# Halves of the first and last pair's keys, scored as they land, in a one-core decode attention kernel

## The chip, the core and the metric

The kernel runs on one core of a Trainium2 chip. A core has five engines with instruction streams of their own: TensorE (PE in the profile), VectorE (DVE), ScalarE (ACT), GpSimd (POOL) and SyncE (SP), which issues nearly all the loads here. Loads go through 16 DMA engines. The metric is the time of one execution in device microseconds, as a median over runs: 693.17 us for the kernel before (three runs, 692.98 to 693.86).

## The reference

One token goes through a conditioned transformer block: a modulated layer norm, attention of 32 heads over a cache of 16384 tokens, the output matrix wo, a second modulated layer norm, and a gated feed-forward part. Cut to what matters:

```python
mod = (_silu(c) @ w_mod).reshape(1, 6, 1, -1)          # sa, ca, ga, sb, cb, gb
h = _layernorm(x) * (1 + ca) + sa
q = (h @ wq)                                           # 32 heads of 128
scores = einsum('bhqd,bhkd->bhqk', q, k_cache) * 128 ** -0.5   # 16384 tokens a head
o = einsum('bhqk,bhkd->bhqd', softmax(scores), v_cache)
x = x + ga * (o @ wo)
h = _layernorm(x) * (1 + cb) + sb
x = x + gb * ((_silu(h @ w_gate) * (h @ w_up)) @ w_down)
```

Everything is bf16; keys and values are 268 MB of the 290 MB that are read.

## The kernel before

**Pairs of heads.** The 32 heads are taken as 16 pairs. Partition `(h q)` of the 128 holds one of the pair's two heads and one of 64 blocks of 256 tokens (`T2 = 256`), so a pair's keys are a tile of 128 partitions x 256 tokens x 128 values, 8.4 MB. Keys live in `kring`, two such buffers used in turn; values in the single buffer `vbuf`. In the text, K0 to K15 and V0 to V15 are the loads of pairs 0 to 15.

**Loads.** All large loads are issued by SP, one after the other on one queue, each after a wait of its own: the keys of pair p + 1 once PE has summed the scores of pair p - 1 (`load_k`, `o_R`), the values of pair p once PE has used those of pair p - 1 (`load_v`, `o_pv`). The order is w_mod, wq, K0, K1, V0, K2, V1, K3, V2 and so on to K15, V14, then wo (two loads, into the first key buffer), V15 in four pieces (`VCUT`), and w_gate, w_up, w_down (into the second key buffer).

**Scores of a pair** (`step`, `score`, `reduce_mm`). DVE multiplies the keys in place by the query (L481), adds the two halves of the 64 products it took (L485, a fold), and folds again (L490). It does so for one half of each row's 128 values (all 256 tokens), then for the other. PE sums what remains over an identity matrix into a PSUM tile: 16 matmuls of 256 columns for each half (L472), 32 in all. So DVE can start a pair only when all its keys have landed.

**Weights and values.** While DVE works on pair p, the scores of pair p - 1 go through their maximum (`largest`: DVE L494, ACT L496, PE L498) and exponentials (`weigh`: DVE L502, ACT L506), and PE multiplies them with the values (`pv`, L445, 64 matmuls), ACT copies the sums (L451), and PE takes out the diagonal blocks (`diag`, L460), which ACT stores as `OT_sb` (L465).

**The tail.** After pair 15's scores come its maximum and weights, a sum of all weights over partitions (L570), its reciprocal (L572), the product with the heads' outputs (L573), a spread of these over columns (`z_op`, L589) and a small matmul with a copy (`lay`, L602, L605) that brings them into the layout of wo's rows, 140 matmuls with wo for the first 28 heads (`project`, L617), the values of pair 15, its diagonal, and 20 matmuls for the last four heads. Then follow the second layer norm, w_gate and w_up (L661) and w_down (L682), and the store.

**Order.** Each engine works in the order in which the program is written. On PE alone, pairs 2 to 15 form a hardware loop of seven rounds with two pairs each (`in_loop`); within it each wait is a semaphore count that grows by a fixed step per round.

Of the kernel before, what the change touches and what calls it, by code (L numbers as in the profile page):

```python
# [8 lines left out]
ALU = mybir.AluOpType  # L9
# [4 lines left out]
class _Chan:  # L14

    def __init__(self, sem, inc):
        self.sem = sem
        self.inc = inc
        self.count = 0

# [16 lines left out]
class _Plan:  # L37
# [54 lines left out]
    def emit(self, block):  # L92
# [5 lines left out]
        for e in self.ENGS:  # L98
            by_place = {}
            for o in per_eng[e]:  # L100
                if o.loop:
                    key, i, n = o.loop
                    by_place.setdefault((key, i), []).append(o)
            for (key, i), ops in by_place.items():
                first = by_place[(key, 0)]
                assert len(first) == len(ops), (key, i)
                for a, b in zip(first, ops):
                    a.sig = a.sig or b.sig
            for (key, i), ops in by_place.items():
                for a, b in zip(by_place[(key, 0)], ops):  # L110
                    b.sig = a.sig
            for o in per_eng[e]:
                if o.sig:
                    ch = o.chan if o.chan is not None else self.chans[e]
                    o.chan = ch
                    ch.count += ch.inc
                    o.val = ch.count
# [7 lines left out]
        def run(name, eng):  # L125
            known = {}
            ops = per_eng[name]
            at = 0
            while at < len(ops):
# [16 lines left out]
                done = {}  # L146
                with eng.Fori(0, n) as it:
                    for b in range(body):
                        each = [self.needs(r[b]) for r in rows]
                        assert all(set(x) == set(each[0]) for x in each), rows[0][b].name  # L150
                        for k, (ch, v0) in each[0].items():
                            step = each[1][k][1] - v0
                            assert all(x[k][1] == v0 + j * step for j, x in enumerate(each)), (rows[0][b].name, [x[k][1] for x in each])
                            if known.get(k, 0) >= each[-1][k][1]:
                                continue
                            if k in done and done[k][1] == step and done[k][0] >= v0:
                                continue
                            done[k] = (v0, step)
                            assert v0 > 0 and step >= 0
                            eng.wait_ge(ch.sem, v0 if step == 0 else it * step + v0)  # L160
                        issue(eng, rows[0][b])
# [28 lines left out]
def build(nc, A_x, A_k, A_v, A_wq, A_wo, B_wg, B_wu, B_wd, c_in, w_mod, out):  # L190
# [20 lines left out]
    with es:  # L211
# [265 lines left out]
        def score(p, c, between=None):  # L477
# [4 lines left out]
                     deps=[d_k[p]] + o_qev[p // 2], name="mult%d_%d" % (p, c))  # L482
# [4 lines left out]
            if between:  # L487
# [3 lines left out]
                      deps=[o_f], name="fold%d_%db" % (p, c))  # L491

# [17 lines left out]

        def step(p):
            f0 = score(p, 0, (lambda: largest(p - 1), lambda: weigh(p - 1)) if p >= 1 else None)
            reduce_mm(p, 0, f0)
            if p >= 1:
                pv(p - 1)
            o_R[p] = reduce_mm(p, 1, score(p, 1))
            if p >= 1:
                diag(p - 1)
# [4 lines left out]
        step(0)  # L523
        load_k(2)
        step(1)
        load_v(1)
        NLOOP = (NP - 2) // 2
        d_wo = {}
        for p in range(2, NP):
            plan.in_loop(LOOP_ON, "pairs", (p - 2) // 2, NLOOP)  # L530
            if p + 1 < NP:
                load_k(p + 1)
            else:
                a = 0
                while a < len(GROUPS):
                    b = a
                    while b < len(GROUPS) and GROUPS[b][1] == GROUPS[a][1]:
                        b += 1
                    (h0, n), h1 = GROUPS[a], GROUPS[b - 1][0] + GROUPS[b - 1][1]
                    d = dma(wo_v[:, h0:h1, :].rearrange("p (g k) n -> p g (k n)", k=n),  # L540
                            A_wo[h0 * 128:h1 * 128, :].rearrange("(g p k) n -> p g (k n)", p=128, k=n),
                            ("wo", a), deps=[o_R[NP - 2]], name="dma_wo%d" % a)
                    for i in range(a, b):
                        d_wo[i] = d
                    a = b
# [8 lines left out]
        wdeps = [o_R[NP - 1]]  # L554
        d_wg = dma(wg_v, B_wg.rearrange("(p k) n -> p k n", p=128), "wg", deps=wdeps, name="dma_wg")
        wu_src = B_wu.rearrange("(p k) n -> p k n", p=128)
        UK = KC - 1
        d_wu = [dma(wu_v[:, 0:UK, :], wu_src[:, 0:UK, :], "wu0", deps=wdeps, name="dma_wu0"),
                dma(wu_v[:, UK:KC, :], wu_src[:, UK:KC, :], "wu1", deps=wdeps, name="dma_wu1")]
        d_wd = []  # L560
        for b in range(NB):
            d_wd.append(dma(wd_v[:, 4 * b:4 * b + 4, :].rearrange("p r n -> p (r n)"),
                            B_wd[512 * b:512 * b + 512, :].rearrange("(p r) n -> p (r n)", r=4), ("wd", b), deps=wdeps, name="dma_wd%d" % b))
        d_wd.append(dma(wd_v[0:FR, 4 * NB:FCH, :].rearrange("p r n -> p (r n)"),
                        B_wd[512 * NB:F, :].rearrange("(p r) n -> p (r n)", r=2), ("wd", NB), deps=wdeps, name="dma_wd%d" % NB))

        LAST = H - 2
        o_Lm = op(PE, lambda e: e.matmul(misc[:, LS0:LS0 + H], lhsT=ones_f[:], rhs=rsz[:], start=True, stop=True),  # L570
                  deps=[o_exp[NP - 1], o_rz, o_onesf, o_rstd], name="L")
        o_rl = op(DVE, lambda e: e.reciprocal(out=rl[:], in_=misc[:, LS0:LS0 + H]), deps=[o_Lm, o_ones1], name="rl")  # L572
        o_on = op(DVE, lambda e: e.tensor_tensor(out=on_f[:, 0:LAST], in0=OT_sb[:, 0:LAST], in1=rl[:, 0:LAST], op=ALU.mult),  # L573
                  deps=[o_rl] + o_ot[0:NP - 1], name="on")
        zoff, zo = [], 0
        for h0, n in GROUPS:
            zoff.append(zo)
            zo += 1
# [45 lines left out]
        for g in range(NG - 1):  # L624
            project(g)

        pv(NP - 1)
# [108 lines left out]
```

## Time and profile before

| | us |
|---|---|
| median of 3 runs | 693.17 |
| the profiled execution | 693.76 |
| its span, by the trace | 692.0 |
| DVE busy | 504.7 (73%) |
| PE busy | 384.1 (55%) |
| ACT busy | 45.8 (7%) |
| data read | 290.47 MB, 420 GB/s over the span |

The span is that of the profiled execution; the numbers worked out from rows below belong to it. In a row of a group of instructions stand line, engine, operation, output and input with their shapes and the count, then the busy time and the mean ns of one, then the idle time of the engine just before them and what ended it. A row of the chain has start, duration and what ran. A row of a window has its bounds and length, the busy time of PE, weight load, DVE, ACT and POOL, the granted clock of TensorE, the mean busy share of the DMA engines and GB/s. A row of loads issued ends with the size in KB and the time from issue to landing in us.

### The profile page before, as it was taken

How to read it: one execution, taken by the hardware profiler on the slowest of the kernel's cores; microseconds unless marked ns; L12 is line 12 of the kernel's file. 1: busy time of each engine (PE TensorE's matmuls, PEld its weight loads, DVE VectorE, ACT ScalarE, POOL GpSimd, SP SyncE). 2: the span in 40 equal slices, each digit the busy share in tenths (PEclk: the TensorE clock that was granted, in tenths of full speed). 3: DMA queues.
4: the chain of work that ended last, by engine and by line, in shares of the span. 5: the costliest groups of instructions: out<-in, count | busy, mean ns of one | idle time of the engine just before them, and what ended most of it. 6: DMA issues, size and time to landing. Idle time of an engine off the chain costs nothing.

```text
span 692.0 us, 5102 instructions
## 1 busy us (share of the span) xinstructions
PE 384.1 (55%) x2280; PEld 154.2 (22%) x2281; DVE 504.7 (73%) x174; ACT 45.8 (7%) x145; POOL 0.7 (0%) x6
## 2 busy tenths in 40 slices
PE   2523457745728284745728184645738173746786
PEld 2311112221302122221212122221212121221355
DVE  2029999959596896959596986959595987959311
ACT  1120000000000000000000000000000000000100
POOL 0000000000000000000000000000000000000000
PEclk9975556565556555565655565655556565555665
DMA  9999899999999999999999999999999999999993
GB/s 388 438 424 425 367 424 417 425 428 426 425 428 462 428 432 432 424 428 447 443 428 432 428 424 428 466 424 428 432 428 424 439 455 428 428 432 404 416 421 120
DMA packets 7135, 290.63 MB, mean 420 GB/s; under 512 B 882, under 2 KB 884, under 8 KB 1876
## 3 DMA queue, kind: packets, MB, share of 16 engines
q1 hardware_dynamic: 7120, 290.48, 97.6%
q8 instruction: 8, 0.13, 0.1%
q14 instruction: 3, 0.02, 0.0%
q10 hardware_dynamic: 4, 0.00, 0.0%
HBM read 290.47 MB, written 0.00 MB: 420 GB/s over the span
## 4 chain that ended last, share of the span: by engine, by line
DMA 45%; DVE 41%; PE 12%; ACT 1%; issue 1%; SPq 0%; DVEq 0%
DMA kring<-in_A_k_cache_dram 45%; DVE kring L481 22%; DVE kring L485 11%; PE psb L472 8%; DVE kring L490 6%; PE psb L617 1%; PE psb L661 1%; PE psb L445 1%; PE psb L682 0%; DVE pm L494 0%; PE psb L460 0%; DVE nb L502 0%; ACT PZ L506 0%; PE psb L602 0%; SPq L79 0%
## 5 line engine op out<-in xcount | busy, mean ns | idle before, releaser
L481 DVE TENSOR_TENSOR kring<-kring,qbc 128x16384 bf16<-128x16384 bf16 x32 | 278.0, 8687 | 126.5 <-DMA kring<-in_A_k_cache_dram 126.5
L472 PE MATMUL psb<-kring,ident 128*128 128x256 bf16 x512 | 225.6, 607 | 159.5 <-DVE kring L490 159.5
L485 DVE TENSOR_TENSOR kring<-kring 128x8192 bf16<-128x8192 bf16 x32 | 141.4, 4420 | 0.6
L472 PEld LDWEIGHTS psb<-kring,ident 128*128 128x128 bf16 x512 | 59.2, 121 | 308.5 <-DVE kring L490 171.2
L445 PE MATMUL psb<-vbuf,PZ 128*8 128x512 bf16 x1024 | 87.9, 516 | 0.5 <-PE psb L445 0.5
L498 PE MATMUL psb<-d,bd_f 128*128 128x64 f32 x32 | 11.0, 447 | 115.7 <-ACT d L496 115.7
L490 DVE TENSOR_TENSOR kring<-kring 128x4096 bf16<-128x4096 bf16 x32 | 73.1, 2286 | 0.6
L445 PEld LDWEIGHTS psb<-vbuf,PZ 128*8 128x8 bf16 x1024 | 28.5, 108 | 64.7 <-issue 55.3
L498 PEld LDWEIGHTS psb<-d,bd_f 128*128 128x128 f32 x32 | 8.0, 310 | 117.9 <-ACT d L496 64.4
L460 PEld LDWEIGHTS psb<-sel,acc_sb 128*128 128x128 f32 x128 | 29.4, 319 | 7.5 <-issue 4.6
L460 PE MATMUL psb<-sel,acc_sb 128*128 128x2 f32 x128 | 26.2, 327 | 0.7 <-ACT acc_sb L451 0.7
L451 ACT ACTIVATE acc_sb<-psb 128x512 f32<-128x512 f32 x16 | 9.6, 597 | 216.0 <-PE psb L445 216.0
L506 ACT ACTIVATE PZ<-psb,nb 64x256 bf16<-64x256 f32 x32 | 15.0, 468 | 63.0 <-DVE nb L502 62.8
L496 ACT ACTIVATE d<-negid,pm 128x64 f32<-128x64 f32 x16 | 5.6, 348 | 151.1 <-DVE pm L494 150.9
L408 PE MATMUL psb<-vbuf,h_col 128*128 128x512 bf16 x39 | 10.6, 442 | 7.9 <-DMA vbuf<-in_A_wq_dram 7.9
L465 ACT ACTIVATE OT_sb<-psb 128x2 f32<-128x2 f32 x15 | 2.6, 172 | 163.0 <-PE psb L460 163.0
L494 DVE TENSOR_REDUCE pm<-psb 128x1 f32<-128x256 f32 x16 | 6.7, 418 | 7.1 <-PE psb L472 7.1
L631 DVE TENSOR_TENSOR on_f<-psb,rl 128x2 f32<-128x2 f32 x1 | 0.2, 160 | 13.9 <-PE psb L460 13.9
L385 PE MATMUL psb<-silu_c,kring 128*128 128x1 bf16 x150 | 6.2, 178 | 4.8 <-DMA kring<-in_w_mod_dram 4.8
L408 PEld LDWEIGHTS psb<-vbuf,h_col 128*128 128x128 bf16 x40 | 4.2, 111 | 14.0 <-DMA vbuf<-in_A_wq_dram 7.6
L385 PEld LDWEIGHTS psb<-silu_c,kring 128*128 128x128 bf16 x150 | 6.1, 131 | 4.9 <-DMA kring<-in_w_mod_dram 4.9
L617 PE MATMUL psb<-A_sb,kring 128*128 128x1 bf16 x160 | 6.7, 178 | 0.6 <-ACT A_sb L605 0.6
(75 smaller groups left out, 62.3 us busy)
## 6 DMA issues: line engine op xcount, KB each, us to landing
vbuf<-in_A_wq_dram SPq DMA_DIRECT2D x1, 5120.0 KB, 27.4
kring<-in_w_mod_dram SPq DMA_DIRECT2D x1, 4800.0 KB, 14.1
vbuf<-in_A_v_cache_dram SPq DMA_DIRECT2D x1, 4096.0 KB, 13.2
kring<-in_A_wo_dram SPq DMA_DIRECT2D x1, 3840.0 KB, 29.1
kring<-in_B_w_gate_dram SPq DMA_DIRECT2D x1, 2160.0 KB, 18.6
vbuf<-in_A_v_cache_dram SPq DMA_DIRECT2D x1, 2048.0 KB, 17.7
kring<-in_B_w_down_dram SPq DMA_DIRECT2D x3, 640.0 KB, 25.2
kring<-in_B_w_up_dram SPq DMA_DIRECT2D x1, 1728.0 KB, 22.3
```

The costliest lines, as they stand in the source:

```text
L385: last = e.matmul(mod_ps[:, m * KC + k:m * KC + k + 1], lhsT=wm_v[:, kd, m * D + k:m * D + D:KC], rhs=silu_c[:, kd:kd + 1], start=(kd == 0 ...
L408: last = e.matmul(q_ps[b][:, 0:512], lhsT=h_col[:, k:k + 1].broadcast_to([128, 128]), rhs=wq_v[:, k, g * 512:(g + 1) * 512], start=(k == 0 ...
L445: last = e.matmul(acc_ps[32 * s:32 * s + 8, :], lhsT=PZ[:, p % 2, j, :], rhs=vbuf[:, 4 * j:4 * j + 4, :].rearrange("p t d -> p (t d)"), st ...
L451: o_acc[p] = op(ACT, lambda e: e.activation(out=acc_sb[:], in_=acc_ps[:], func=ACTF.Copy), deps=[o_pv[p], o_diag[p - 1] if p >= 1 else Non ...
L460: last = e.matmul(OT_ps[:, 0:2], lhsT=acc_sb[:, 128 * i:128 * (i + 1)], rhs=sel[:, i:8:4], start=(i == 0), stop=(i == 3))
L472: last = e.matmul(S_ps[p % 2][:, 0:T2], lhsT=ident[:], rhs=kring[:, p % 2, :, d], start=(d == 0), stop=(d == QW + QR - 1))
L481: o_m = op(DVE, lambda e: e.tensor_tensor(out=kv4, in0=kv4, in1=q4, op=ALU.mult), deps=[d_k[p]] + o_qev[p // 2], name="mult%d_%d" % (p, c))
L485: o_f = op(DVE, lambda e: e.tensor_tensor(out=kv4[:, :, 0], in0=kv4[:, :, 0], in1=kv4[:, :, 1], op=ALU.add), deps=[o_m], name="fold%d_%d" ...
L490: return op(DVE, lambda e: e.tensor_tensor(out=lo[:, :, 0:QR], in0=lo[:, :, 0:QR], in1=lo[:, :, QR:QW], op=ALU.add), deps=[o_f], name="fol ...
L498: o_mx[p] = op(PE, lambda e: e.matmul(mx_ps[:, 0:64], lhsT=bd_f[:], rhs=d2[:], start=True, stop=True), deps=[o_d2, o_bd1, o_bd2, o_nb[p - ...
L506: o_exp[p] = op(ACT, lambda e, half=half, ps=ps: e.activation(out=PZ[ps, p % 2, :, 4 * half:4 * half + 4], in_=S_ps[p % 2][ps, 0:T2].rearr ...
L617: last = e.matmul(attn_ps[:, cc:cc + 1], lhsT=wo_v[:, k, cc:D:KC], rhs=A_sb[:, k:k + 1], start=(k == 0 and cc == 0), stop=(k == H - 1 and ...
```

## The change

For pairs 0 and 15 (`ENDS`), the keys come in two loads of 128 tokens a partition each (`KCUT`), with a semaphore of their own. A new `score_end` works on one such half: the product of whole rows of 128 values with the query, then three folds (to 64, 32 and 16 values); a new `reduce_end` sums a half with 16 matmuls of 128 columns. The pairs between are as before.

Pair 15 moves out of the loop. Its steps are written out, with pair 14's maximum, weights, values and diagonal between them. The sum of weights is split: that for the first 30 heads (`La`, with its reciprocal `rla`, the product, the spreads and the lays of the first four groups) is placed ahead of pair 15's maximum; that for the last two heads (`Lb`, `rlb`) comes after pair 15's weights. The 140 matmuls with wo stay after pair 15's weights. PE's loop covers pairs 1 to 14, again seven rounds; `emit` now works out each wait's first count from the second and third round, and puts a wait that only the first round needs ahead of the loop.

```diff
+        ENDS = (0, NP - 1)
+        KCUT = [0, T2 // 2, T2]
...
         def load_k(p):
             deps = [o_R[p - 2]] if p >= 2 else ([o_mod] if p == 1 else [])
-            d_k[p] = dma(kring[:, p % 2], k_src(p), ("k", p % 2), deps=deps, name="dma_k%d" % p)
+            cuts = KCUT if p in ENDS else [0, T2]
+            d_k[p] = [dma(kring[:, p % 2, a:b], k_src(p)[:, a:b], ("k", p % 2, c), deps=deps, name="dma_k%d_%d" % (p, c))
+                      for c, (a, b) in enumerate(zip(cuts, cuts[1:]))]
...
+        def score_end(p, c, between=None):
+
+            kv = kring[:, p % 2, KCUT[c]:KCUT[c + 1]]
+            o = op(DVE, lambda e: e.tensor_tensor(
+                out=kv, in0=kv, in1=qbc[:, p, :].unsqueeze(1).broadcast_to([128, KCUT[c + 1] - KCUT[c], 128]), op=ALU.mult),
+                deps=[d_k[p][c]] + o_qev[p // 2], name="mult%d_%d" % (p, c))
+            for i, w in enumerate((64, 32, 16)):
+                if between and i < 2:
+                    between[i]()
+                o = op(DVE, lambda e, w=w: e.tensor_tensor(out=kv[:, :, 0:w], in0=kv[:, :, 0:w], in1=kv[:, :, w:2 * w], op=ALU.add),
+                       deps=[o], name="fold%d_%d_%d" % (p, c, w))
+            return o
+
+        def reduce_end(p, c, fold):
+            def f_R(e):
+                last = None
+                for d in range(16):
+                    last = e.matmul(S_ps[p % 2][:, KCUT[c]:KCUT[c + 1]], lhsT=ident[:], rhs=kring[:, p % 2, KCUT[c]:KCUT[c + 1], d],
+                                    start=(d == 0), stop=(d == 15))
+                return last
+            return op(PE, f_R, deps=[fold, o_ident, o_exp[p - 2] if p >= 2 else None], name="R%d_%d" % (p, c))
...
-        step(0)
-        load_k(2)
-        step(1)
-        load_v(1)
+        reduce_end(0, 0, score_end(0, 0))
+        o_R[0] = reduce_end(0, 1, score_end(0, 1))
         NLOOP = (NP - 2) // 2
...
-        for p in range(2, NP):
-            plan.in_loop(LOOP_ON, "pairs", (p - 2) // 2, NLOOP)
+        for p in range(1, NP - 1):
+            plan.in_loop(LOOP_ON, "pairs", (p - 1) // 2, NLOOP)
+            load_k(p + 1)
             step(p)
             load_v(p)
         plan.out_of_loop(LOOP_ON)
-        largest(NP - 1)
-        weigh(NP - 1)
...
+        PL = NP - 1
         LAST = H - 2
-        o_Lm = op(PE, lambda e: e.matmul(misc[:, LS0:LS0 + H], lhsT=ones_f[:], rhs=rsz[:], start=True, stop=True),
-                  deps=[o_exp[NP - 1], o_rz, o_onesf, o_rstd], name="L")
-        o_rl = op(DVE, lambda e: e.reciprocal(out=rl[:], in_=misc[:, LS0:LS0 + H]), deps=[o_Lm, o_ones1], name="rl")
+        f0 = score_end(PL, 0, before(PL))
+        reduce_end(PL, 0, f0)
+        pv(PL - 1)
+        load_v(PL)
+        diag(PL - 1)
+        o_La = op(PE, lambda e: e.matmul(misc[:, LS0:LS0 + LAST], lhsT=ones_f[:], rhs=rsz[:, 0:LAST], start=True, stop=True),
+                  deps=[o_exp[PL - 1], o_rz, o_onesf, o_rstd], name="La")
+        f1 = score_end(PL, 1)
+        o_R[PL] = reduce_end(PL, 1, f1)
+        o_rla = op(DVE, lambda e: e.reciprocal(out=rl[:, 0:LAST], in_=misc[:, LS0:LS0 + LAST]), deps=[o_La, o_ones1], name="rla")
...
         NG = len(GROUPS)
         lay(list(range(NG - 1)))
+        largest(PL)
+        weigh(PL)
+        o_Lb = op(PE, lambda e: e.matmul(misc[:, LS0 + LAST:LS0 + H], lhsT=ones_f[:], rhs=rsz[:, LAST:H], start=True, stop=True),
+                  deps=[o_exp[PL], o_rla], name="Lb")
+        o_rl = op(DVE, lambda e: e.reciprocal(out=rl[:, LAST:H], in_=misc[:, LS0 + LAST:LS0 + H]), deps=[o_Lb, o_ones1], name="rlb")
```

The loads of wo, w_gate, w_up and w_down keep their places among the loads.

More of the change, by code (lines that the diff above doesn't have):

```diff
@@ L147, in run @@
                 with eng.Fori(0, n) as it:
                     for b in range(body):
[L149 to L159, printed above, removed]
+                        for ch, v0, step in body_needs[b]:
@@ L509, in weigh, with before @@
                     deps=[o_nb[p], o_R[p], o_pv[p - 2] if p >= 2 else o_pz, o_rz], name="exp%d_%d" % (p, half))
+        def before(p):
+            return (lambda: largest(p - 1), lambda: weigh(p - 1))
         def step(p):
[L512 to L515, printed above, removed]
+            reduce_mm(p, 0, score(p, 0, before(p)))
+            pv(p - 1)
             o_R[p] = reduce_mm(p, 1, score(p, 1))
-            if p >= 1:
-                diag(p - 1)
+            diag(p - 1)
         load_k(0)
```

88 lines of the change are left out of this document (54 added, 34 removed).

## The prediction

> **What bounds the kernel now.** I read the page first (share of the DMA queue, chain by line, groups), then the chain in order of time, then the issues of the SP queue.
>
> ```profile
> span 692.0 us, 5102 instructions
> q1 hardware_dynamic: 7120, 290.48, 97.6%
> DMA 45%; DVE 41%; PE 12%; ACT 1%; issue 1%; SPq 0%; DVEq 0%
> L481 DVE TENSOR_TENSOR kring<-kring,qbc 128x16384 bf16<-128x16384 bf16 x32 | 278.0, 8687 | 126.5 <-DMA kring<-in_A_k_cache_dram 126.5
> L485 DVE TENSOR_TENSOR kring<-kring 128x8192 bf16<-128x8192 bf16 x32 | 141.4, 4420 | 0.6
> L490 DVE TENSOR_TENSOR kring<-kring 128x4096 bf16<-128x4096 bf16 x32 | 73.1, 2286 | 0.6
> L472 PE MATMUL psb<-kring,ident 128*128 128x256 bf16 x512 | 225.6, 607 | 159.5 <-DVE kring L490 159.5
> ```
>
> The one data queue is busy for 97.6% of the span, while VectorE waits 126.5 us for keys, so one stream of loads bounds the middle. The chain's 41% on DVE misleads there: a pair of DVE work follows each late key load, and the next load is still landing. Two stretches are not bound by the stream: the start and the end. The chain's first multiplication of a pair shows when its keys had landed:
>
> ```profile
> 47.97 8.70 DVE kring L481
> 78.83 8.60 DVE kring L481
> 149.09 8.69 DVE kring L481
> 227.25 8.69 DVE kring L481
> 304.65 8.69 DVE kring L481
> 614.26 8.69 DVE kring L481
> ```
>
> From pair 7 (304.65) to pair 15 (614.26) are 309.61 us and 16 loads of keys or values: 19.35 us a load, the stream's pace. From pair 0 (47.97) to pair 3 (149.09) five loads land (K1, V0, K2, V1, K3) and should take 96.75; they take 101.12, 4.37 too many. From pair 3 to pair 5 four loads take 78.16 in place of 77.40, 0.76 too many. So 5.13 us of the stream are lost at the start. The SP queue and the windows say where:
>
> ```profile
> 85.98 0.33 SPq L79 DMA_DIRECT2D kring<-in_A_k_cache_dram  x1
> 106.78 0.33 SPq L79 DMA_DIRECT2D vbuf<-in_A_v_cache_dram  x1
> 83.00:87.00 4.00, 2.94 (x7) 0.62 (x5) 4.00 (x1) 0.00 (x0) 0.00 (x0) 0.50 0.37 131
> 106.00:107.00 1.00, 0.73 (x16) 0.10 (x8) 1.00 (x1) 0.21 (x1) 0.00 (x0) 1.00 0.00 0
> ```
>
> K2 goes out at 85.98, when PE has finished pair 0's sums; V0 has landed by 47.97 + 2 x 19.35 = 86.7, and some of the 16 engines run dry before that (DMA share 0.37). V1 goes out at 106.78, when the values of pair 0 have been used; K2 is just running out (0.00 in that microsecond). Both issues are late because DVE scores pair 0 only from 47.97.
>
> At the end the last keys are there at 614.26, and a chain of DVE, PE and ACT follows that outlasts the stream:
>
> ```profile
> 645.40 7.05 PE psb L472 x16
> 656.76 0.65 PE psb L570 x2
> 659.48 5.76 PE psb L617 x140
> 665.24 3.26 PE psb L445 x17
> 670.82 0.41 PE psb L445 x4
> 671.25 0.61 ACT acc_sb L451
> 671.90 1.07 PE psb L460 x8
> 688.04 0.55 PE psb L682 x10
> ```
>
> **The change part by part.**
>
> *A third fold.* A half of the tokens with whole rows has the same 16384 products as a half of the rows before, then folds of 8192, 4096 and now 2048. The folds' means give 0.521 ns an element ((4420 - 2286)/4096), so 2048 elements cost 2.286 - 1.067 = 1.22 us. Bounds: 1.14 (half of L490's) and 2.29 (all of it); I take 1.22. A half then takes 8.69 + 4.42 + 2.29 + 1.22 = 16.6 us, 33.2 an end pair where it was 30.8.
>
> *Sums on PE.* Two times 16 matmuls of 128 columns in place of 32 of 256. One of 256 costs 0.44 us (7.05/16); the one-column matmuls of L617 follow each other at 0.041, so columns make about 0.40 of the 0.44, and 128 columns cost 0.24: 3.8 us a half. Bounds: 3.5 (half of 7.05) and 7.05 (nothing saved).
>
> *Two loads in place of one.* Half of K0 lands half a pace earlier, at 47.97 - 9.7 = 38.3. The price of a cut is in V15, which already comes in four:
>
> ```profile
> kring<-in_A_wo_dram SPq DMA_DIRECT2D x1, 1280.0 KB, 31.7
> vbuf<-in_A_v_cache_dram SPq DMA_DIRECT2D x1, 2048.0 KB, 17.7
> vbuf<-in_A_v_cache_dram SPq DMA_DIRECT2D x1, 1536.0 KB, 21.0
> vbuf<-in_A_v_cache_dram SPq DMA_DIRECT2D x1, 512.0 KB, 22.1
> kring<-in_B_w_down_dram SPq DMA_DIRECT2D x1, 240.0 KB, 26.9
> 613.78 0.92 SPq L79 DMA_DIRECT2D kring<-in_A_wo_dram  x2
> 642.49 1.79 SPq L79 DMA_DIRECT2D vbuf<-in_A_v_cache_dram  x4
> L79 SPq DMA_DIRECT2D kring<-in_B_w_down_dram x4: 432/438/3191, 653.8 to 655.2; - x4
> ```
>
> Issues plus times to landing: of two wo issues in 0.92 the second is at 614.2 and lands at 614.2 + 31.7 = 645.9; of V15's four in 1.79, each 0.45 after the other, the last is at 643.8 and lands at 643.8 + 22.1 = 665.9. V15 took 20.0 where one load takes 19.35, so a cut costs (20.0 - 19.35)/3 = 0.2 us. Bounds 0 and 0.65; I take 0.2 for K0 and 0.2 for K15. The Trainium skill (DMA: Bandwidth & Descriptors, Anatomy of one DMA) puts about 2.0 us of fixed cost on every load, measured there on another issue path; by it the two cuts cost 4.0 and the sum below ends 3.6 us higher. The pieces of V15 contradict it for loads queued behind each other, so I keep 0.2.
>
> *Front, with these.* Scoring pair 0 runs 38.3 to 54.9 and 54.9 to 71.5 (its second half landed at 48), PE's sums end at 75.3: K2 goes out 10.7 us earlier, 9 before the first engines run dry. DVE starts pair 1 at 71.5 in place of 78.83, as K1 is there by 47.97 + 19.35 = 67.3; PE's work follows, so V1 goes out 7.3 earlier, at 99.5, while K2 lands at 47.97 + 3 x 19.35 = 106.0. K3 and V2 follow 110 and 134, against landings of 125 and 145. Nothing is late next but the stream itself: DVE is free at 102.6 and waits for K2. So the whole 5.13 goes, less 0.2 for the cut: **-4.9 us**. The price if the cover is gone: engines finish up to some 3 us ahead of a load's landing (they were dry for most of 83 to 87, with V0 landing at 86.7), so V1 has 3.5 us to spare, and each us beyond comes back.
>
> *The loop on PE* covers pairs 1 to 14 in place of 2 to 15, still seven rounds. Its first round waits on counts worked back from the second; only the first maximum's wait is stricter than need be, on pair 0's first half of scores, done 25 us before. Cost nothing. The order of the loads on SP is unchanged; only POOL is untouched altogether.
>
> *Tail*, in the times of before (the stream carries all of them 4.9 earlier). Rows on which it rests:
>
> ```profile
> 604.35 2.29 DVE L490 TENSOR_TENSOR kring<-kring 128x4096 bf16<-128x4096 bf16 x1
> 636.99 5.46 PE L445 MATMUL psb<-vbuf,PZ 128*8 128x512 bf16 x64
> 652.27 1.68 PE L460 MATMUL psb<-sel,acc_sb 128*128 128x2 f32 x8
> 672.00:674.00 2.00, 1.22 (x11) 1.05 (x12) 0.39 (x2) 0.17 (x1) 0.00 (x0) 1.00 0.93 389
> ```
>
> Half of K15 is there at 604.6, DVE is free at 606.65: it starts 7.6 us earlier. First half with the maximum and minimum of pair 14 (0.5): 623.7; second: 640.3. On PE the first sums end at 627.5, and pair 14's values now wait behind them for V14, at 614.24 + 19.35 = 633.6: 5.5 us to 639.1, copy 0.6, diagonal 1.7, the early sum of weights 0.65: 642.1. Only then can the second sums run, 3.8 us to 645.9, where before they ended at 652.45. The early reciprocal, product and spreads (1.6 us on DVE) lie beside these sums; the four lays and their copy (1.0) now stand ahead of the last maximum on PE and ACT. Maximum to the sum of weights took 652.45 to 657.41, 5.0; with up to 0.5 of the lays uncovered: 651.4. wo has landed (645.9), its 140 matmuls take 5.76: 657.2, where before 665.24. Then V15, piece by piece: first half 3.3 to 660.5; the second piece lands at 642.9 + 17.7 = 660.6 and takes 1.06, the third at 643.35 + 21.0 = 664.4 and takes 0.85, the fourth at 665.9 and takes 0.41: 666.3 where it was 671.23. So PE is 4 us ahead of V15's last pieces, and the landing is the end: 4.9 us earlier, not 8. With nothing saved on PE's sums (7.05) it is still hidden.
>
> What follows is unchanged, 671.25 to 692.0. One doubt: pair 15's diagonal took 1.07 at a granted clock of 1.00 (the figure before the DMA share in the last row), pair 14's took 1.68, and PE now idles between V15's pieces: 0 to 0.6, I take 0.3. The weights don't hold it: the last of them lands at 655.2 + 26.9 = 682.1, and its ten matmuls come at 688.04 - 4.6 = 683.4. More than 5.9 us could not be gained here. **-4.6 us.**
>
> *Sum.* 693.76 (span 692.0 and 1.76 around it) - 4.9 - 4.6 + 0.2 for the cut of K15: 684.5 for the profiled execution. The median of the runs is 693.17, 0.6 lower: 683.9.
>
> **The rivals.**
>
> One end only. If K2 and V1 still start late (say, a queue that takes up new work slowly whatever the issue), only the tail gains: 693.2 - 4.4 = 688.8. If PE's second sums come so late that V15 has long landed, only the front: 693.2 - 4.9 + 0.2 = 688.5. Against the first, the two windows without traffic stand exactly at the late issues; against the second, 4 us of slack.
>
> A price per load. If each cut costs 2 us of the stream, 683.9 + 3.6 = 687.5. For it, 0.65 was lost over V15's three cuts; against it, that is 0.2 each. The fixed cost of the Trainium skill named above would act so.
>
> Slower: the new forms on DVE. They differ from those measured: rows of 128 against a row repeated per token, a fold of 16 elements a token. The reductions show the other pace of this engine:
>
> ```profile
> L494 DVE TENSOR_REDUCE pm<-psb 128x1 f32<-128x256 f32 x16 | 6.7, 418 | 7.1 <-PE psb L472 7.1
> L502 DVE TENSOR_REDUCE nb<-psb 128x1 f32<-128x64 f32 x16 | 3.5, 217 | 2.4 <-PE psb L498 2.4
> ```
>
> (418 - 217)/192 = 1.05 ns an element, twice 0.521. At that pace a half (16384 + 8192 + 4096 + 2048 elements) costs 30720 x 0.53 = 16.3 us more, an end pair 32.6. K2 would go out at 75.3 + 32.6 = 107.9, 21.9 later than now, and V1 at 132, 4 after K2's landing: some 22 more lost than today. In the tail the second sums start 30.8 late, less 4 of slack and the 4.6 gained: 22 again, near 737. It decides once an end pair costs some 9 us more: 3.5 of it are covered in front and 5.8 in the tail, the rest counts twice. Against it: type and step inside a row are those of the old forms, whose rows were shorter.
>
> No change would take a wait I haven't seen on the front and the tail alike.
>
> **Chances.** Forecast 0.78, one end only 0.09, price per load 0.05, slower 0.06, no change 0.02 (within 0.2%, about what a measurement of this kernel can tell). Faster 0.92, same 0.02, slower 0.06. The forecast's own bounds are 683.9 - 0.4 (cuts) - 0.3 (clock) - 0.9 (lays and weights) = 682.3 and 683.9 + 1.3 (cuts at 0.65, clock) + 0.8 (the 0.76 between pairs 3 and 5 stays) = 686.0. With the price per load the range is 682.3 to 687.6.
>
> **What would show it.** Right: pair 0's first multiplication near 38; K2 out near 75 and V1 near 100; no window of no traffic before 110; pairs 3 and 5 starting near 144.5 and 222; the last pair's sums ending near 641; PE waiting for V15's pieces, the last four of its matmuls at landing; end 20.7 after. Wrong: multiplications or folds off 8.69, 4.42, 2.29, 1.22; the two K0 loads over 19.6 together; the second sums waiting on something other than pair 14's diagonal; a gap in PE between project and values that V15 doesn't explain.

## The result, and the profile after

The changed kernel takes 686.58 us (median of four runs, 686.2 to 686.8), the kernel before 693.51 beside it (four runs, 692.98 to 693.93). The ratio is 0.99, 95% interval 0.9883 to 0.9917: 6.9 us are gained. The forecast was 683.9 in a range of 682.3 to 687.6, so the time lies in the range, 2.7 us above the forecast. The forecast's own bounds ended at 686.0; the time lies 0.6 beyond them, in the part of the range that only the rival of a price per load had opened. The profiled execution took 686.55, its span is 684.6 (684.56), 7.48 shorter than the span before (692.04).

From the page of the changed kernel, the lines that answer those shown of before: span, the data queue (packets, MB, share), the chain's shares, and the groups of DVE and PE with busy time, mean ns and the idle time before them.

```profile
span 684.6 us, 5113 instructions
q1 hardware_dynamic: 7408, 290.48, 98.4%
DMA 52%; DVE 35%; PE 12%; issue 0%; ACT 0%; SPq 0%; DVEq 0%
L503 DVE TENSOR_TENSOR kring<-kring,qbc 128x16384 bf16<-128x16384 bf16 x28 | 243.3, 8689 | 95.0 <-DMA kring<-in_A_k_cache_dram 95.0
L518 DVE TENSOR_TENSOR kring<-kring,qbc 128x16384 bf16<-128x16384 bf16 x4 | 34.7, 8687 | 16.2 <-DMA kring<-in_A_k_cache_dram 16.2
L532 PE MATMUL psb<-kring,ident 128*128 128x128 bf16 x64 | 14.5, 393 | 35.9 <-DVE kring L524 35.9
```

The data queue is busy for 98.4% of a shorter span, and VectorE waits 111 us for keys (95.0 + 16.2) where it waited 126.5. The product over whole rows (L518) takes 8687 ns, exactly what the old form took. The chain in order of time, with start, duration and what ran:

```profile
38.13 8.70 DVE kring L518
46.85 4.44 DVE kring L524
51.31 2.30 DVE kring L524
53.64 1.23 DVE kring L524
54.86 8.62 DVE kring L518
...
71.57 3.64 PE psb L532 x16
```

And line L503, the product for the pairs between, from 140 to 230 us, with the count, the shortest, median and longest in ns, and the first and last start:

```profile
L503 DVE TENSOR_TENSOR kring<-kring,qbc x5: 8685/8692/8693, 144.7 to 222.1; 128x16384 bf16<-128x16384 bf16 x5
```

Pair 0 starts at 38.13 where it started at 47.97; pair 3 at 144.7 (149.09 before), pair 5 at 222.1 (227.25). The issues on SP's queue and the windows in which nothing was moved before:

```profile
75.22 0.33 SPq L80 DMA_DIRECT2D kring<-in_A_k_cache_dram  x1
99.07 0.33 SPq L80 DMA_DIRECT2D vbuf<-in_A_v_cache_dram  x1
```

```profile
83.00:87.00 4.00, 0.00 (x0) 0.00 (x0) 4.00 (x3) 1.12 (x4) 0.00 (x0) 0.50 1.18 508
106.00:107.00 1.00, 1.00 (x4) 0.36 (x3) 1.00 (x1) 0.00 (x0) 0.00 (x0) 0.50 1.52 655
```

K2 goes out at 75.22 and V1 at 99.07, and both windows are full of traffic. (A packet counts whole in the window in which it starts, so the share of a short window can pass 1.) That is the front's gain. The tail, in PE's rows (start, busy time, idle time before the row and what ended it):

```profile
634.92 1.05 PE L482 MATMUL psb<-sel,acc_sb 128*128 128x2 f32 x8 [0.70 <-ACT acc_sb L473]
...
636.06 3.64 PE L532 MATMUL psb<-kring,ident 128*128 128x128 bf16 x16
639.53 0.27 PE L630 MATMUL psb<-e,Z 128*128 128x8 bf16 x4
...
643.22 5.72 PE L645 MATMUL psb<-A_sb,kring 128*128 128x1 bf16 x140
650.71 3.59 PE L467 MATMUL psb<-vbuf,PZ 128*8 128x512 bf16 x32 [1.76 <-DMA vbuf<-in_A_v_cache_dram]
655.61 1.88 PE L467 MATMUL psb<-vbuf,PZ 128*8 128x512 bf16 x16 [1.31 <-DMA vbuf<-in_A_v_cache_dram]
659.30 1.45 PE L467 MATMUL psb<-vbuf,PZ 128*8 128x512 bf16 x12 [1.81 <-DMA vbuf<-in_A_v_cache_dram]
660.91 0.60 PE L467 MATMUL psb<-vbuf,PZ 128*8 128x512 bf16 x4 [0.16 <-PE psb L467]
662.21 1.87 PE L482 MATMUL psb<-sel,acc_sb 128*128 128x2 f32 x8 [0.70 <-ACT acc_sb L473]
```

PE now waits for the landing of three of V15's pieces. The last piece landed at 660.48, but its four matmuls start only at 660.91, behind those of the third: so the end of the tail is set by the third piece's landing and by PE's pace behind it. ACT's copy of pair 15's sums (L473) starts at 661.56 where it started at 671.25: 9.69 us earlier, 9.6 had been forecast. But the span is only 7.48 shorter. Two things give back 2.2 us behind that copy. The diagonal takes 1.87 us where it took 1.07, and the product behind it begins 2.62 us after the start of ACT's copy, where it was 1.75. And the store, the last transfer, takes longer. Its row (size in KB, us from issue to landing) in the kernel before:

```profile
out_dram<-o_col SPq DMA_DIRECT2D x1, 1.2 KB, 2.6
```

and in the changed kernel:

```profile
out_dram<-o_col SPq DMA_DIRECT2D x1, 1.2 KB, 4.0
```

By the trace's landings it is 2.65 before (issued 689.00, landed 691.65) and 3.98 after (680.19 and 684.17): 1.33 us more for the same 1.2 KB. The sum: 9.69 - 0.87 - 1.33 = 7.49, the span's 7.48. Between the diagonal's product and the last addition nothing moved (15.81 against 15.82 us).

### The profile page after: what moved, and what is told of

It reads as the page before. It is cut to its first block, busy times and chain, and to the rows that moved or that the text cites. A ratio compares the mean times of both kernels' runs of the same rounds, so it can differ in the third digit from the quotient of the medians.

```text
span 684.6 us, 5113 instructions
## 1 busy us (share of the span) xinstructions
PE 366.3 (54%) x2282; PEld 152.5 (22%) x2283; DVE 509.8 (74%) x179; ACT 45.8 (7%) x145; POOL 0.7 (0%) x6
## 3 DMA queue, kind: packets, MB, share of 16 engines
q1 hardware_dynamic: 7408, 290.48, 98.4%
## 4 chain that ended last, share of the span: by engine, by line
DMA 52%; DVE 35%; PE 12%; issue 0%; ACT 0%; SPq 0%; DVEq 0%
DMA kring<-in_A_k_cache_dram 44%; DVE kring L503 16%; DVE kring L507 8%; DMA vbuf<-in_A_v_cache_dram 8%; PE psb L494 7%; DVE kring L512 4%; DVE kring L518 3%; DVE kring L524 2%; PE psb L467 2%; PE psb L709 1%; PE psb L532 1%; PE psb L730 0%; DVE pm L538 0%; PE psb L482 0%; SPq L80 0%
## 5 line engine op out<-in xcount | busy, mean ns | idle before, releaser
L503 DVE TENSOR_TENSOR kring<-kring,qbc 128x16384 bf16<-128x16384 bf16 x28 | 243.3, 8689 | 95.0 <-DMA kring<-in_A_k_cache_dram 95.0
L494 PE MATMUL psb<-kring,ident 128*128 128x256 bf16 x448 | 197.4, 607 | 124.1 <-DVE kring L512 124.1
L507 DVE TENSOR_TENSOR kring<-kring 128x8192 bf16<-128x8192 bf16 x28 | 123.8, 4420 | 0.5
L467 PE MATMUL psb<-vbuf,PZ 128*8 128x512 bf16 x1024 | 84.6, 500 | 11.7 <-DMA vbuf<-in_A_v_cache_dram 11.5
L512 DVE TENSOR_TENSOR kring<-kring 128x4096 bf16<-128x4096 bf16 x28 | 64.0, 2287 | 0.5
L518 DVE TENSOR_TENSOR kring<-kring,qbc 128x16384 bf16<-128x16384 bf16 x4 | 34.7, 8687 | 16.2 <-DMA kring<-in_A_k_cache_dram 16.2
L532 PE MATMUL psb<-kring,ident 128*128 128x128 bf16 x64 | 14.5, 393 | 35.9 <-DVE kring L524 35.9
L524 DVE TENSOR_TENSOR kring<-kring 128x8192 bf16<-128x8192 bf16 (+2 forms) x12 | 31.7, 2646 | 0.3
L473 ACT ACTIVATE acc_sb<-psb 128x512 f32<-128x512 f32 x16 | 9.6, 597 | 222.2 <-PE psb L467 222.2
```

What stands on the lines that cost most here:

```text
L467: last = e.matmul(acc_ps[32 * s:32 * s + 8, :], lhsT=PZ[:, p % 2, j, :], rhs=vbuf[:, 4 * j:4 * j + 4, :].rearrange("p t d -> p (t d)"), st ...
L494: last = e.matmul(S_ps[p % 2][:, 0:T2], lhsT=ident[:], rhs=kring[:, p % 2, :, d], start=(d == 0), stop=(d == QW + QR - 1))
L503: o_m = op(DVE, lambda e: e.tensor_tensor(out=kv4, in0=kv4, in1=q4, op=ALU.mult), deps=[d_k[p][-1]] + o_qev[p // 2], name="mult%d_%d" % (p ...
L507: o_f = op(DVE, lambda e: e.tensor_tensor(out=kv4[:, :, 0], in0=kv4[:, :, 0], in1=kv4[:, :, 1], op=ALU.add), deps=[o_m], name="fold%d_%d" ...
L512: return op(DVE, lambda e: e.tensor_tensor(out=lo[:, :, 0:QR], in0=lo[:, :, 0:QR], in1=lo[:, :, QR:QW], op=ALU.add), deps=[o_f], name="fol ...
L518: o = op(DVE, lambda e: e.tensor_tensor(out=kv, in0=kv, in1=qbc[:, p, :].unsqueeze(1).broadcast_to([128, KCUT[c + 1] - KCUT[c], 128]), op= ...
```

## Experiments

Each ratio is to the kernel before in runs on the same chip. That kernel had medians of 693.49 (13 runs), 694.0 (7), 693.99 (17) and 693.86 (13) in the four sets below.

**Each end alone.** Both gains are worked out separately in the forecast, so each half of the change should show its own.

```diff
 # front only: pair 15 by step() with whole keys, one sum of weights behind its weights
-        ENDS = (0, NP - 1)
+        ENDS = (0,)
...
-        f0 = score_end(PL, 0, before(PL))
-        reduce_end(PL, 0, f0)
-        pv(PL - 1)
+        step(PL)
         load_v(PL)
-        diag(PL - 1)
+        largest(PL)
+        weigh(PL)
...
```

> The changed kernel with its tail as before (last pair's keys in one load, scored by halves of rows with two folds, one sum of weights after the last pair's). Theory (the front's gain is the stream's 5.1 us, and it reaches the end whole): pair 15 starts 5.1 earlier than in the kernel before, the copy of pair 15's sums near 666.1 in place of 671.25, time near 688.4; near 689.7 if the store takes the 1.3 us more that the changed kernel shows. Rival (the whole gain stems from the tail, what the front gains is lost on the way): near 693.5. Rival (front and tail overlap): 686.6.

```diff
 # tail only: pair 0 with whole keys
-        ENDS = (0, NP - 1)
+        ENDS = (NP - 1,)
...
-        reduce_end(0, 0, score_end(0, 0))
-        o_R[0] = reduce_end(0, 1, score_end(0, 1))
+        reduce_mm(0, 0, score(0, 0))
+        o_R[0] = reduce_mm(0, 1, score(0, 1))
```

> The changed kernel with its front as before (first pair's keys in one load, scored by halves of rows). Theory: the stream stands as in the kernel before (pair 15's keys all landed near 614.2), the copy of pair 15's sums is near 666.7 in place of 671.25, the diagonal loses 0.9 to a half clock: time near 689.8 with the store as before, near 691.1 with the slower store. So e1 and e2 add up to the whole. Rival (the tail's gain hangs on the front's): 693.5.

Measured: 691.29 us for the front alone (five runs, 689.75 to 691.76; ratio 0.996, 0.9946 to 0.9974), 691.79 for the tail alone (nine runs, 691.02 to 692.5; 0.9975, 0.9965 to 0.9985). In medians they gain 2.2 and 1.7, together 3.9, where the whole change gains 6.9. So two expectations missed: both medians lie above what was expected even with a slower store (689.7 and 691.1), and the halves do not add up to the whole. The traced executions are the slowest of their kernels (691.76 and 692.5); two of the five runs of the front alone, 689.75 and 689.79, are where it was expected. The profiles say what the traced ones lost. With the front alone K2 goes out at 75.32 and V1 at 100.44, with the tail alone at 85.95 and 107.50 as before, and there the window behind V1's late issue is empty again:

```profile
107.00:108.00 1.00, 0.45 (x12) 0.00 (x0) 0.97 (x2) 0.49 (x1) 0.00 (x0) 1.00 0.01 0
```

The front does what was forecast and does it alone: with it, the last weights land at 676.9 where they land at 682.2 before, 5.3 earlier; without it, they land at 682.4 and the empty microsecond is back. What is lost lies in the tail. PE's rows with the front alone:

```profile
660.14 3.59 PE L467 MATMUL psb<-vbuf,PZ 128*8 128x512 bf16 x32
663.89 1.88 PE L467 MATMUL psb<-vbuf,PZ 128*8 128x512 bf16 x16 [0.16 <-PE psb L467]
665.93 0.83 PE L467 MATMUL psb<-vbuf,PZ 128*8 128x512 bf16 x12 [0.16 <-PE psb L467]
```

Here PE is late and not the landing (no wait on a DMA), and its first 48 matmuls take 5.47 us where they took 4.33 (3.29 and 1.04). The copy on ACT comes 3.88 us earlier (667.37), where the stream's 5.14 would have put it at 666.11: 1.26 is lost. The store takes 4.54, 1.89 more than before: 692.04 - 5.14 + 1.26 + 1.89 = 690.05, the span's 690.04. With the tail alone the copy comes 4.15 earlier, the diagonal takes 1.87, from the copy to the store's issue pass 18.64 us where it was 17.75, and the store takes 4.17: 692.04 - 4.15 + 0.89 + 1.52 = 690.30, the span's 690.3. So both halves pay for a slow store, which the whole change pays once; and in these two executions each loses around 1 us to PE running slower, the front alone ahead of the copy, the tail alone in the diagonal.

**The split sum of weights undone.** The change also brings the sum of the first 30 heads' weights, their reciprocal, product and lays ahead of the last pair's maximum.

```diff
-        o_La = op(PE, ... rsz[:, 0:LAST] ...)
         f1 = score_end(PL, 1)
         o_R[PL] = reduce_end(PL, 1, f1)
-        o_rla = op(DVE, ... rl[:, 0:LAST] ...)
+        largest(PL)
+        weigh(PL)
+        o_La = op(PE, ... rsz[:] ...)          # all 32 heads
+        o_rla = op(DVE, ... rl[:] ...)
```

> The changed kernel with one sum of all weights, its reciprocal, product, spreads and lays after the last pair's weights, as before. Theory (PE waits for V15's pieces at the end, so 2 to 3 us more ahead of the matmuls with wo are covered): no change, 686.6 within 0.3; the wait for V15's first piece shrinks from 1.8 to nothing. Rival (the early sums carry part of the tail's gain): 688.5 to 689.3.

Measured: 686.54 (686.22 to 686.72; 0.9901, 0.9886 to 0.9916) beside 686.58 for the change. PE's rows:

```profile
646.17 5.76 PE L647 MATMUL psb<-A_sb,kring 128*128 128x1 bf16 x140 [0.28 <-ACT A_sb L635]
...
659.34 1.45 PE L467 MATMUL psb<-vbuf,PZ 128*8 128x512 bf16 x12 [2.65 <-DMA vbuf<-in_A_v_cache_dram]
```

The matmuls with wo start 2.95 us later (646.17 for 643.22), and the third piece of V15 still starts at 659.34 (659.30), after a wait for its landing. The copy starts at 661.60 (661.56). The split brings nothing, because PE has the slack. So the tail's gain comes with the halves of K15 and not with the split.

**PE kept busy while it waits for V15.** The diagonal at 1.07 or 1.87 looked like the granted clock. In the changed kernel's windows (the columns are bounds, length, busy time of PE, weight load, DVE, ACT, POOL, then the clock, the DMA share, GB/s):

```profile
643.00:649.00 6.00, 5.95 (x142) 5.86 (x142) 0.17 (x1) 0.00 (x0) 0.00 (x0) 0.50 1.01 431
650.00:654.00 4.00, 3.29 (x32) 0.95 (x32) 0.00 (x0) 0.00 (x0) 0.00 (x0) 0.50 1.00 424
...
662.00:664.00 2.00, 1.79 (x8) 1.78 (x8) 0.00 (x0) 0.16 (x1) 0.00 (x0) 0.50 0.99 422
```

the clock is 0.50 in each, where the window of before with the diagonal in it had 1.00. To test it, matmuls of 512 columns that nobody reads (into an idle PSUM bank) go ahead of the first three pieces, sized to PE's waits:

```diff
+        FILL = (4, 6, 6)
...
+                if p == NP - 1 and c < 3:
+                    fill(FILL[c])
                 prev = op(PE, f_pv, deps=[o_exp[p], d_v[p][c], ...
```

> The changed kernel with 4, 6 and 6 matmuls of 512 columns, whose result nobody reads, before the first three of V15's four pieces, so that PE does not idle there. Theory (the end lost 0.9 us on the diagonal and 0.5 on the last pieces because the granted clock fell to half while PE waited): clock 1.0 from about 656 on, the diagonal 1.07 in place of 1.88, time 1.0 to 1.4 lower, near 685.4. Rival (the longer diagonal has another cause): 686.6, or up to 2 higher where the added matmuls delay the pieces.

Measured: 685.7 (four runs, 685.03 to 686.05; 0.9887, 0.9871 to 0.9902), 0.9 lower in the median than the change, but the intervals of the two ratios overlap, so that the gain is likely and not shown. PE's rows and windows:

```profile
656.64 1.04 PE L478 MATMUL psb<-vbuf,PZ 128*8 128x512 bf16 x16
657.61 1.47 PE L466 MATMUL psb<-PZ,ident 128*128 128x512 bf16 x6
659.45 0.82 PE L478 MATMUL psb<-vbuf,PZ 128*8 128x512 bf16 x12 [0.38 <-DMA vbuf<-in_A_v_cache_dram]
660.71 0.39 PE L478 MATMUL psb<-vbuf,PZ 128*8 128x512 bf16 x4 [0.44 <-DMA vbuf<-in_A_v_cache_dram]
661.80 1.71 PE L495 MATMUL psb<-sel,acc_sb 128*128 128x2 f32 x8 [0.70 <-ACT acc_sb L486]
```

```profile
658.00:662.00 4.00, 2.48 (x23) 0.79 (x21) 0.00 (x0) 0.60 (x1) 0.00 (x0) 1.00 1.05 443
662.00:664.00 2.00, 1.52 (x8) 1.43 (x7) 0.34 (x2) 0.00 (x0) 0.00 (x0) 0.50 0.99 423
```

The clock is full, the three later pieces take 1.04, 0.82 and 0.39 where they took 1.88, 1.45 and 0.60, and the last of them waits for its landing again. The diagonal stays slow, as the clock falls to 0.50 at 662.01, 0.2 us after it began. So the pieces were slow for the clock; the diagonal is settled two steps below.

**The kernel before, twice more.** The store's landing in two more traces of the unchanged kernel, to see whether 2.65 was a lucky draw:

> The kernel before, unchanged, for a second trace. In the first one its store landed 2.65 us after its issue, in the changed kernel 3.98, in e1, e2, e3 and e4 4.54, 4.17, 3.75 and 4.29. Theory (the store's landing scatters by some 2 us from execution to execution, and the first trace had a short one): between 3.5 and 4.6 here. Rival (it belongs to the program, and the change made it longer): 2.6 to 2.8 again.

> The same kernel once more, with the same two expectations; and, as the granted clock's windows lie otherwise in each execution, pair 15's 64 matmuls with values take between 5.5 and 7.5 us from one trace to the next (theory: the end of the kernel before already depends on that by up to 2 us).

Measured: 2.95 and 2.67 us (single times 694.57 and 692.07). Three traces of the kernel before give 2.65 to 2.95; the changed kernel and the four variants above 3.75 to 4.54. It isn't scatter: the slow store belongs to the program. The values of pair 15 took 5.86 and 5.46 us of busy PE in these traces, beside 5.54 in the first: the speed of PE in the tail varies a little in the kernel before too, though by far less than the 2 us that had been thought possible.

**A further step: wo's second load behind V15.** With the landing of V15 as the end, 1.3 MB of wo for the heads 24 to 31 can come after it, with 20 matmuls moved behind the diagonal.

```diff
-        # both loads of wo ahead of V15
+        load_wo(0, 3)
...
         load_v(PL)
+        load_wo(3, 5)
...
-        for g in range(NG - 1):
+        for g in range(NG - 2):
             project(g)
         pv(NP - 1)
         diag(NP - 1)
+        project(NG - 2)
```

> The changed kernel with the second load of wo (heads 24 to 31, 1.3 MB, 3.0 us of the stream) behind V15 in place of ahead of it, and the matmuls of heads 24 to 27 behind pair 15's diagonal. Theory (the end follows V15's last landing by a fixed chain, not the stream's end): V15's last piece lands 3.0 earlier, near 657.4, the time falls by 2 to 2.5 (the last weights, near 676.4, then stop a part of it): near 684.3. Rival (the stream's end, with the last weights, sets the end): 686.6.

> e7 with 8, 8, 2 and 2 matmuls of 512 columns that nobody reads ahead of V15's second, third and fourth piece and of the diagonal. Theory of the clock: the diagonal and the last pieces at a clock of 1.0, up to 1.3 less than e7, of which the last weights stop a part: 683.3 to 684.3. Rival: as e7, or more by what the added matmuls delay.

(The second adds such idle matmuls as above, 8, 8 and 2 ahead of the later pieces of V15 and 2 ahead of the diagonal.) Measured: 684.95 (684.66 to 685.41; 0.9866, 0.9842 to 0.989), and 685.45 with the matmuls (684.62 to 686.4; 0.9875, 0.9848 to 0.9901). The first is the fastest kernel of the study: 9.0 us below the kernel before beside it (694.0), and 1.6 below the median of the changed kernel, of which it shares no run's time (684.66 to 685.41, 686.2 to 686.8). In the first, ACT's copy comes 3.0 us earlier than in the changed kernel (658.57), but only 1.4 of it reaches the store's issue (678.77 for 680.19). PE's rows in the second kernel show what is next:

```profile
658.72 1.05 PE L497 MATMUL psb<-sel,acc_sb 128*128 128x2 f32 x8 [0.17 <-ACT acc_sb L488]
660.76 0.96 PE L658 MATMUL psb<-A_sb,kring 128*128 128x1 bf16 x20 [0.99 <-DMA kring<-in_A_wo_dram]
...
670.10 2.35 PE L723 MATMUL psb<-h_col,kring 128*128 128x1 bf16 x56 [0.65 <-DMA kring<-in_B_w_up_dram]
...
675.48 0.96 PE L744 MATMUL psb<-gu_col,kring 128*128 128x1 bf16 x20 [0.89 <-DMA kring<-in_B_w_down_dram]
677.05 1.64 PE L744 MATMUL psb<-gu_col,kring 128*128 128x1 bf16 x30 [0.61 <-DMA kring<-in_B_w_down_dram]
```

Two readings. The diagonal takes 1.05 at a granted clock of 1.00, so the forecast's doubt is settled: it was the clock. And what PE saves is now handed to the stream: PE waits for wo, w_up and w_down (0.99, 0.65, 0.89, 0.61). From here the end of the stream is the bound, and the idle matmuls show no gain (685.45 for 684.95, with overlapping intervals).

**Where the slow store comes from.** Two kernels that split the change the other way: the kernel before with only the load of K0 cut, and the changed program with neither end cut.

```diff
 # kernel before, K0 in two loads, scored only when both are there
+            cuts = [0, T2 // 2, T2] if p == 0 else [0, T2]
-            d_k[p] = dma(kring[:, p % 2], k_src(p), ("k", p % 2), ...)
+            d_k[p] = [dma(kring[:, p % 2, a:b], k_src(p)[:, a:b], ("k", p % 2, c), ...)
+                      for c, (a, b) in enumerate(zip(cuts, cuts[1:]))]
...
-                     deps=[d_k[p]] + o_qev[p // 2], ...
+                     deps=d_k[p] + o_qev[p // 2], ...
```

> The kernel before with one edit: the keys of pair 0 come in two loads by tokens, and the first multiplication waits for both, so that nothing is scored earlier. Pair 0 starts when its keys have landed, at 47.9 us as before, and the stream, the tail and the weights' last landing (682.2) stay. What is open is the landing of the store, 2.65 to 2.95 us after its issue in three traces of the kernel before, 3.75 to 4.54 in every kernel in which K0 or K15 is cut. Theory A, the added load on SP's queue does it: 3.8 to 4.5 us from issue to landing, and a time of 694.5 to 695. Theory B, the rest of the rewritten program does it (the pairs' loop moved by one, another order of instructions): 2.65 to 2.95 us, and a time of 693.5 as before.

```diff
 # changed program, no end cut (the tail as in the front-only kernel)
-        ENDS = (0, NP - 1)
+        ENDS = ()
```

> The changed program with neither end cut: pairs 1 to 14 in the loop as in the changed kernel, pair 0 ahead of it and pair 15 behind it, but both with whole loads and the half scores by dimensions, and one sum of weights behind pair 15's, as in the kernel before. Loads start as before (K2 near 86, V1 near 107), the weights' last landing stays near 682.2. Theory A, an added load makes the store land later: there is none, so 2.65 to 2.95 us from issue to landing, and 693.5 as before. Theory B, the rewritten program does it: 3.8 to 4.5 us, and 694.5 to 695. If both kernels of this call have the short landing or both the long one, neither theory stands alone.

Measured: the cut alone 695.34 (nine runs; 1.0026, 1.0014 to 1.0038), slower than the kernel before; the rewritten program without cuts 693.12 (ten runs; 0.9993, 0.998 to 1.0005), the same. The store takes 3.96 us in the first, 2.83 in the second. So the move of the loop costs nothing, and one added load, by which nothing is scored earlier (pair 0 starts at 47.86), costs about 1.3 us by the medians (695.34 for 693.99) at the end of the kernel, 640 us after it has landed. Page lines of the cut alone, the data queue's packets and the store:

```profile
q1 hardware_dynamic: 7264, 290.48, 97.5%
...
out_dram<-o_col SPq DMA_DIRECT2D x1, 1.2 KB, 4.0
```

The added load makes 144 packets (7264, where the kernel before has 7120). Two kernels then ask whether it is the number of loads or where the cut is made, and whether it is SP's queue.

```diff
 # K0 cut as above, and w_up in one load: as many loads as in the kernel before
-        d_wu = [dma(wu_v[:, 0:UK, :], ..., "wu0", ...),
-                dma(wu_v[:, UK:KC, :], ..., "wu1", ...)]
+        d_wu = [dma(wu_v, wu_src, "wu0", ...)] * 2
```

> The kernel before with pair 0's keys in two loads that the first multiplication waits for (e9_k0_cut_alone: store 3.96 us, 695.34), and w_up in one load instead of two, so that SP's queue carries as many loads ahead of the store as in the kernel before. w_up has landed long before its sums in the kernel before, so that this should move nothing else. Theory A, the number of loads on the queue decides: 2.65 to 2.95 us from issue to landing, and 693.5 to 694.0 as in the kernel before. Theory B, the cut of the first keys does it, wherever the count stands: 3.8 to 4.5 us, and 695.3.

```diff
 # the kernel with wo's second load late, and the store issued by ScalarE
-        d_out = dma(out..., o_col[:], "out", deps=[o_oc], name="dma_out")
+        d_out = dma(out..., o_col[:], "out", deps=[o_oc], name="dma_out", eng="act")
```

> The kernel with wo's second load behind V15 (e7_wo_late, 684.95 us), with the store issued by ScalarE instead of SyncE, so that it goes into the queue that has carried only the two small loads of the start. Theory A, the number of loads on SP's queue ahead of the store makes it land late: 2.65 to 2.95 us from issue to landing instead of 4.53, and 683.2 to 683.5 us. Theory B, the store lands late in every program that has more loads, whichever queue it takes: 3.75 to 4.5 us, and 684.9 as without the edit. ScalarE waits for VectorE's last addition as SyncE does, so that the issue should stand where it stood, 678.8.

Measured: with w_up whole 693.71 (ten runs; 1.0, 0.999 to 1.0009), the loss of the cut is gone. Its lines:

```profile
q1 hardware_dynamic: 7120, 290.48, 97.7%
...
out_dram<-o_col SPq DMA_DIRECT2D x1, 1.2 KB, 2.7
```

The store through ScalarE's queue: 685.29 (four runs, 684.83 to 685.46; 0.9874, 0.9855 to 0.9894), not told apart from 684.95 without the edit, and the store is slow there as well:

```profile
out_dram<-o_col ACTq DMA_DIRECT2D x1, 1.2 KB, 4.1
```

| kernel | loads and store, both queues | store, issue to landing, us |
|---|---|---|
| before (three traces) | 49 | 2.65, 2.95, 2.67 |
| loop alone | 49 | 2.83 |
| K0 cut, w_up whole | 49 | 2.67 |
| K0 cut alone | 50 | 3.96 |
| front only, tail only | 50 | 4.54, 4.17 |
| the change; one sum; busy PE | 51 | 3.98, 3.75, 4.29 |
| wo late; with busy PE; store on ScalarE | 51 | 4.53, 4.29, 4.07 |

In the table, five traces at 49 transfers have 2.65 to 2.95, nine with 50 or 51 have 3.75 to 4.54. The store is slow on either queue, and with the added load at K0 or at K15. Of the theories, the number of loads holds, though not as the store's place on SP's queue; it is that of the program.

The traces say one thing more about where the time goes. The store's 144 packets are through 1.06 to 1.50 us after its issue in the nine traces with the long landing and 1.06 to 1.94 in the five others, so they do not go out later. The landing is told by 16 steps of the store's semaphore, and these come later: in the changed kernel the packets are through at 681.25 and the steps come from 682.13 to 684.17; in the kernel before the packets are through at 690.51 and the steps come from 690.30 to 691.65.

Why is open. Each added load also brought 144 packets and a semaphore of its own, and with it another number for the store's semaphore: 122 in all five traces with the short landing, 123 or 124 in the nine with the long one. No run tells these apart. By the table, removing two loads from the changed kernel should bring its 1.3 us back, but that wasn't tried.

## Why the prediction was right, and what it mis-sized

*The front.* Right in every step: pair 0's first multiplication at 38.13 (38.3 forecast), K2 out at 75.22 (75.3), V1 at 99.07 (99.5), pairs 3 and 5 at 144.7 and 222.1 (144.5 and 222), no empty window. The stream gains 5.15 by pair 5's start, all of the 5.13 that the rows of before showed as lost. The front-only run shows that it needs nothing of the tail.

*The third fold* took 1.23 (1.22), PE's sums 3.64 a half (3.8). VectorE kept its pace in the new forms, so the slower rival falls with its first condition.

*Two loads in place of one.* The 0.2 a cut was too much as a price of the stream: V15's last piece and the last weights land 5.4 and 5.8 us earlier, more than the front's 5.1, so nothing was charged for either cut there. With it falls the rival of 2 us of the stream a load. The fixed cost that the Trainium skill (DMA: Bandwidth & Descriptors, Anatomy of one DMA) gives for another issue path does not show here for loads queued behind each other. But the step missed another price, since it asked only what a cut does to the stream: the store lands 1.33 us later once the program has more loads. This is the largest error of the sum, and no row of the trace of before had shown it.

*The tail.* The mechanism was right in the main: pair 14's diagonal at 634.92 holds the second sums back, they run 636.06 to 639.7 (an end near 641 was forecast), the 140 matmuls end near 649 and PE waits for V15. The slack forecast on PE was 4 us, and the run with one sum of weights used 3 of it without loss. ACT's copy came 9.69 earlier for 9.6, but that this fits so well is in part luck. The last piece landed at 660.48, 0.7 ahead of the 661.2 that the forecast comes to (665.9 - 4.9 + 0.2), and its matmuls started 0.43 behind the landing and took 0.60 for 0.41: two errors of 0.7 and 0.6 that cancel. The sign "the last four of its matmuls at landing" did not come; it did in the run with PE kept busy (landing 660.67, start 660.71).

*The doubt on the clock* was real, and its size was the second error. It had been put at 0.3, within 0 to 0.6, for the diagonal alone. The diagonal and what follows to its product took 0.87 more. The pieces ahead of it ran at half clock too; with the clock up, the third and fourth piece take 0.84 less. What the forecast gave to the landing alone was in part PE's pace.

*The end 20.7 after the copy* was 23.0 (684.56 - 661.56): 0.87 of it the diagonal, 1.33 the store.

*The sum.* The forecast for the profiled execution was 684.5, it took 686.55: 1.33 for the store, 0.57 for the clock (0.87 - 0.3), 0.1 back by the copy, 0.23 for what lies around the span (1.99 for 1.76). The other 0.6 of the 2.7 came from setting the median 0.6 under the profiled execution, as it was before the change; after it they agree to 0.03. That the time still lies in the range is owed to room that was left for another reason: the 2 us a cut were to be lost in the stream, where nothing was lost, and the 1.33 came at the store, of which the prediction said nothing.

## What to carry to other kernels

Find where the load stream runs dry at its ends, from issues that wait for compute, and start compute on a part of a load: rows of the trace gave the front's gain to 0.1 us. Then ask what replaces the old bound behind it. Here, with PE waiting for data in the tail, the granted clock stayed at 0.50, and a short stage behind the waits took 1.87 us; with matmuls of 512 columns in the gaps it took 1.05. And an added transfer may cost nothing where it stands and still something elsewhere: look at the last store's landing in every variant.

## What was not expected of the hardware

- With one more load, hidden in the stream, the final 1.2 KB store lands 0.8 to 1.9 us later: 2.65 to 2.95 us in five traces with 49 transfers, 3.75 to 4.54 in nine with 50 or 51, whichever queue issues the store. Its packets go out no later; the steps of the semaphore that tell of the landing come later.
- One-column matmuls kept PE busy without raising its clock: 5.95 us of PE in 6 us (643 to 649) at 0.50. With matmuls of 512 columns it rose: in the run with them the clock was full from 655.18 to 662.01, 6.83 us. The Trainium skill (TensorE: Matmul & The Clock Gate, Part 1) has the clock rise after about 3.4 us of activity and fall after an idle window of that length. The spells of full clock seen here, 3.41, 6.83 or 10.24 us long, agree with its window; but busy by the profile's count of PE was not enough here.
